# A recurrent scan with a top-1 mixture of experts on one core: second matrices kept on chip and addressed through a TensorE register

## The chip, the cores and the metric

The kernel runs on one core of one Trainium2 chip. The metric is the device time of one execution in microseconds (us). The times of the kernel before are the median, lowest and highest of three runs. The trace is of one more execution, taken by the hardware profiler.

## The reference, cut to what matters

```python
# part 1: x, r_gate, i_gate are 4 x 5056 x 256
a_t = exp(8 * sigmoid(r_gate) * log(sigmoid(a_param)))
x_gated = sqrt(max(1 - a_t*a_t, 1e-6)) * sigmoid(i_gate) * x
h[t] = a_t[t] * h[t-1] + x_gated[t]          # along the 5056 steps
# part 2: the 20224 rows of h (256 wide), 8 experts of 256 -> 1024 -> 256
e = argmax(h @ w_gate);  p = softmax(h @ w_gate)[e]
out = p * (relu(h @ w1[e]) @ w2[e])
```

## The kernel before, in words

The 20224 tokens are 158 blocks of 128, taken in 40 quads of up to four blocks. The program goes through these steps, with the names that its functions, and the lines below, have.

**Front of a quad.** ScalarE (ACT) computes tanh, exp and square root (L638 to L666), VectorE (DVE) multiplies and scans along time (L655, L671, L690). TensorE (PE) forms the gate logits (`lp`, L709), turns them (`lt`, L724) and transposes the scanned rows (`yt`, L747). ACT and DVE write each row as two fp16 parts, high and low (`hi` L774, `lw` L781), into `rows`.

**Routing.** Quads are taken in groups (`GROUPS`). For one group DVE finds each token's expert and gate weight (`r1` to `r6`, L796 to L857), PE counts places (`rk`, L815 and L816), and GpSimd (POOL) sends each block's rows with an indirect DMA to the region of their expert in `buf` in DRAM (`scat`, L870). A fence on SyncE (SP) tells that a group has landed.

**Slots.** The experts then work on slots of 256 or 128 rows of one expert. SP loads meta data and, by a DMA transpose, the rows (`xL`, L1061 and L1068). PE multiplies with the first matrix (`L1`, L1110), ACT applies relu (L1122), DVE makes the low part (L1130), PE multiplies with the second matrix (`L2`, L1149 to L1151), ACT scales (`ot`, L1160), and POOL stores the rows with an indirect DMA (`store`, L1171). In fp16 each product has three terms, high by high, high by low and low by high; this gives 48 matmuls for L1 and 48 for L2 in a slot of 256 rows (256 columns each), and 48 of 128 columns with 24 of 256 columns in a slot of 128 rows.

**The first eight slots, one for each expert,** are called raw: they use the fp32 matrices as they came, 32 and 32 matmuls in the trace (L1110, L1147) for 256 rows. The rows of the first two (`PICK = 2`) don't come by way of DRAM: DVE makes selection matrices for each block of the first four quads (`sel`, L892), PE multiplies them with `rows` (`pick`, L904), and ACT copies the product out of PSUM (`xs`, L910). The other six are read back from `buf`, and POOL joins their two parts (L1081). Meanwhile each of the 16 matrices is prepared for fp16: a sum of its magnitudes on ACT or DVE (`wm`, L956), the scale (`wt` on PE, L962, and `ws`), the high part on ACT (`wh`, L976), the low part on DVE (`wl`, L981), and a store into `wscr` in DRAM (`wr`).

**Later slots** are taken from tables that the device computes, so which expert a slot has is known only in a register. For each slot SP loads both prepared matrices (1 MB each) from `wscr` at an address of its registers (L1038), unless the buffer holds that expert already; POOL multiplies the gate weights with the scales of both matrices (`f`, L1093). There are `NB = 4` pairs of buffers.

The order of every engine's instructions is fixed when the program is built, by a planner (`Plan`): it runs its own model of the engines, takes the ready task with the best priority (`URGE`, `PREP`, `EARLY` and others), and counts the buffers in `BUFS`. On the chip the engines then wait for each other through semaphores, and each engine works its list in order.

## Time and profile before

| | |
|---|---|
| median of 3 runs | 1061.1 us (1059.38 to 1061.73) |
| the profiled execution | 1071.31 us, its span 1069.5 us, mean granted TensorE clock 0.988 |
| PE busy | 990.3 us (93% of the span), 8854 matmuls recorded |
| weight loads of PE, DVE, ACT, POOL busy | 860.6, 688.3, 616.8, 422.4 us |
| moved by DMA | 305.72 MB, mean 286 GB/s |

The span is read in four stretches. Up to the first L1 at 80.6 us ACT and DVE work on the first four quads and PE waits. From there to about 225 us the raw slots run while matrices are prepared. From there to 1032 us the slots from the tables run while the other quads are scanned and routed. The last 37 us are slots alone, and the stores of the last rows.

### The profile page before, as it was taken

The page shows a single profiled execution, that of the slowest core. Times are in us where ns is not written, and L with a number is a line of the kernel's source. Part 1 is how long each engine was busy: PE and PEld are TensorE (multiplying, and loading weights), DVE is VectorE, ACT ScalarE, POOL GpSimd, SP SyncE. Part 2 cuts the span into 40 slices and gives each one's busy share as a digit, 9 for nine tenths or more (in the row PEclk, how much of TensorE's full clock was granted, in tenths as well). Part 3 has the DMA queues.
Part 4 walks back from the last instruction along what each step waited for, and adds up shares of the span by engine and source line. Part 5 has one row for each costly group of instructions (what it writes and reads, how often), then busy time and mean ns, then how long its engine had stood idle before and what let it go on. Part 6 is the DMA issues. An engine that isn't in the chain of part 4 may idle for free. (4 is left out here: it accounts for less than half of the span.)

```text
span 1069.5 us, 23793 instructions
## 1 busy us (share of the span) xinstructions
PE 990.3 (93%) x8854; PEld 860.6 (80%) x8854; DVE 688.3 (64%) x1448; ACT 616.8 (58%) x815; POOL 422.4 (39%) x498
## 2 busy tenths in 40 slices
PE   1369898989899999999999999999999999999997
PEld 1138787878778888888888888888888888889987
DVE  4898898886676666758667585765858464422221
ACT  8988785664837466664755747466674632222222
POOL 0154454333446434353544525345253434222222
PEclk9979999999999999999999999999999999999999
DMA  9977998989998989799899989969899997878881
GB/s 366 380 241 213 324 336 282 299 281 327 331 332 245 316 275 356 208 343 308 263 323 309 345 267 316 295 199 350 303 348 297 279 316 195 238 241 267 224 245 54
DMA packets 167028, 305.72 MB, mean 286 GB/s; under 512 B 117621, under 2 KB 117754, under 8 KB 145659
## 3 DMA queue, kind: packets, MB, share of 16 engines
q1 hardware_dynamic: 151450, 262.56, 77.5%
q0 software_dynamic: 15456, 41.60, 12.2%
q8 instruction: 70, 1.15, 0.4%
q14 instruction: 52, 0.42, 0.1%
HBM read 251.48 MB, written 63.91 MB: 295 GB/s over the span
## 5 line engine op out<-in xcount | busy, mean ns | idle before, releaser
L1110 PE MATMUL p<-xT,wt 128*128 128x256 f16 (+1 forms) x3936 | 414.7, 263 | 8.3 <-DMA wt<-wscr 6.1
L1110 PEld LDWEIGHTS <-wt 128*128 128x128 f16 x3936 | 353.9, 98 | 48.1 <-DMA wt<-wscr 6.9
L1130 DVE SCALAR_TENSOR_TENSOR hb<-p,hb 128x1024 f16<-128x1024 f32 x148 | 180.7, 1221 | 238.7 <-ACT hb L1122 217.9
L1171 POOL DMA_INDIRECT out<-ot,meta x164 | 179.4, 1094 | 383.6 <-ACT ot L1160 340.8
L1149 PE MATMUL po<-wt,hb 128*128 128x256 f16 x1184 | 322.8, 273 | 7.9 <-ACT ot L1160 6.9
L1150 PE MATMUL po<-wt,hb 128*128 128x256 f16 x1184 | 322.8, 273 | 0.9 <-issue 0.9
L1151 PE MATMUL po<-wt,hb 128*128 128x256 f16 x1184 | 322.8, 273 | 0.1
L1122 ACT ACTIVATE hb<-p 128x1024 f16<-128x1024 f32 (+1 forms) x164 | 167.0, 1018 | 206.6 <-PE p L1110 170.0
L870 POOL DMA_INDIRECT buf<-rows,pi x158 | 169.7, 1074 | 49.3 <-issue 35.0
L1160 ACT ACTIVATE ot<-po,f 128x256 f32<-128x256 f32 x148 | 69.7, 471 | 170.5 <-PE po L1151 110.5
L1150 PEld LDWEIGHTS <-hb 128*128 128x128 f16 x1184 | 115.8, 98 | 22.9 <-issue 9.5
L1149 PEld LDWEIGHTS <-hb 128*128 128x128 f16 x1184 | 115.7, 98 | 15.5 <-issue 1.3
L1151 PEld LDWEIGHTS <-hb 128*128 128x128 f16 x1184 | 115.8, 98 | 14.5 <-issue 1.1
L690 DVE TENSOR_TENSOR_SCAN in_x<-in_r,in_x 128x512 f32<-128x512 f32 (+7 forms) x82 | 96.6, 1189 | 1.3
L1093 POOL TENSOR_SCALAR f<-meta,wt,wt 128x2 f32<-128x2 f32 (+1 forms) x82 | 38.3, 468 | 130.3 <-DMA wt<-wscr 93.8
L781 DVE SCALAR_TENSOR_TENSOR rows<-yt,sc,rows 128x256 f16<-128x256 f32 x154 | 65.3, 476 | 5.3 <-ACT rows L774 2.6
L655 DVE SCALAR_TENSOR_TENSOR in_x<-in_i,in_x 128x1024 f32<-128x1024 f32 (+1 forms) x38 | 46.0, 1214 | 34.8 <-ACT in_i L649 26.3
L774 ACT ACTIVATE rows<-yt,sc 128x256 f16<-128x256 f32 x154 | 61.9, 475 | 5.0 <-DVE sc L766 5.0
L1147 PE MATMUL po<-wt,hb 128*128 128x256 f32 x256 | 63.3, 398 | 0.9 <-ACT ot L1158 0.7
L671 DVE SCALAR_TENSOR_TENSOR in_x<-in_i,in_x 128x1024 f32<-128x1024 f32 (+1 forms) x38 | 45.6, 1200 | 24.9 <-ACT in_i L666 22.9
L1110 PE MATMUL p<-x,wt 128*128 128x256 f32 x256 | 58.3, 382 | 0.7 <-ACT x L910 0.7
L1147 PEld LDWEIGHTS po<-wt,hb 128*128 128x128 f32 x256 | 49.0, 198 | 8.7 <-ACT ot L1158 1.5
(126 smaller groups left out, 912.0 us busy)
## 6 DMA issues: line engine op xcount, KB each, us to landing
wt<-wscr SPq DMA_DIRECT2D x164, 1024.5 KB
in_x<-in_rix SPq DMA_DIRECT2D x39, 512.0 KB
in_r<-in_rix SPq DMA_DIRECT2D x37, 512.0 KB
in_i<-in_rix SPq DMA_DIRECT2D x37, 512.0 KB
wscr<-hl SPq DMA_DIRECT2D x16, 1024.5 KB
wt<-in_w SPq DMA_DIRECT2D x16, 1024.0 KB
out<-ot,meta POOLq DMA_INDIRECT x164
buf<-pad SPq DMA_DIRECT2D x10, 258.0 KB
```

Of the source, the lines that this page charges most:

```text
L690: V.tensor_tensor_scan(y[:, lo:hi], av[:, lo:hi], y[:, lo:hi], init, ALU.mult, ALU.add)
L781: V.scalar_tensor_tensor(r[:, 2 * p + j, D:2 * D], o["yt", p][:, j], o["sc"][:, 2 * p + j:2 * p + j + 1], r[:, 2 * p + j, 0:D], ALU.mult, ...
L870: i = G.indirect_dma_start(out=buf[:, :], out_offset=bass.IndirectOffsetOnAxis(ap=g["pi"][:, b0 + j:b0 + j + 1], axis=0), in_=rows[q]["row ...
L1110: T.matmul(pv[:, i], wv[:, wl, kk, fs], o["xT"][:, 2 * xl + kk, 0:U], start=(z == 0), stop=(z == len(seq) - 1))
L1122: A.activation(o["h"][:, gs, 0:U] if o["raw"] else o["h"][:, 0, gs, 0:U], o["p1", g], AF.Relu)
L1130: V.scalar_tensor_tensor(o["h"][:, 1, gs, 0:U], o["p1", g], 0.0, o["h"][:, 0, gs, 0:U], ALU.max, ALU.subtract)
L1147: T.matmul(dst, h[:, f, ts], wv[:, f, :], start=(f == 0), stop=(f == NF - 1))
L1149: T.matmul(dst, h[:, 0, f, ts], wv[:, 0, f, :], start=(f == 0), stop=False)
L1150: T.matmul(dst, h[:, 0, f, ts], wv[:, 1, f, :], start=False, stop=False)
L1151: T.matmul(dst, h[:, 1, f, ts], wv[:, 0, f, :], start=False, stop=(f == NF - 1))
L1160: A.activation(o["ot", j], o["po", j], AF.Copy, scale=o["f2"][:, j:j + 1])
L1171: i = G.indirect_dma_start(out=out[:, :], out_offset=bass.IndirectOffsetOnAxis(ap=o["id"][j], axis=0), in_=o["ot", j], in_offset=None, bou ...
```

## The change

**Second matrices.** All eight prepared second matrices lie side by side in one tile `w2all` on chip. For each slot PE itself loads the expert's number into one of its registers (`second`), and every matmul of L2 takes its moving operand at an address computed from that register (`times`). From `wscr` only the first matrix is loaded, 1 MB for a slot, into `NB = 5` single buffers; the scales of both matrices travel with it. A raw second matrix is loaded into the place of the next expert's prepared one.

**First slots.** The raw slots of experts 0 to 2 have 128 rows, picked from the first two quads alone (`NEAR = 3`, `PASSES`); experts 3 to 7 have 256 rows, read from `buf` after quads 2 and 3. The picking has 32 matmuls of 384 columns (before 64 of 512) and 24 selection matrices of 128 columns for a quad (before 16 of 256).

**Elsewhere.** `GROUPS` are all of two quads; the sums `wm` of nine matrices are on ACT (before six), each in two halves; fewer buffers for several tiles (`rows` 4 to 2, `xT` 4 to 2, `ot` 9 to 2, `hl` 2 to 1, `x32` 6 to 3); other priorities, hence another order on every engine.

```diff
-NB = 4
+NB = 5
-PASSES = ((1, 256, 8),)
+PASSES = ((0, 128), (1, 256), (2, 256))
-SUMS = (0, 6)
+SUMS = (0, 9)
-PICK = 2
+NEAR = 3
...
-BUFS = dict(r=3, i=4, x=6, rows=4, yt=2, lp=1, rank=1, tot=1, lg=4, hl=2, xT=4, hb=3, ot=9, po=1, p1=2, reg=3, x32=6)
+BUFS = dict(r=3, i=2, x=4, rows=2, yt=2, lp=1, rank=1, tot=2, lg=4, hl=1, xT=2, hb=3, ot=2, po=1, p1=2, reg=3, x32=3)
...
-            cond = None if was is None or was[1] else o["er"] != was[0]
-            nc.sync.dma_start(t, wscr[bass.ds(o["er"], 1), i].rearrange("a p c -> p (a c)"), cond=cond)
+        nc.sync.dma_start(t, wscr[bass.ds(o["er"], 1)].rearrange("a p c -> p (a c)"), cond=None if was is None else o["er"] != was)
+
+    def second(o):
+
+        z = st["tab", o["z"]]["ti"][:, 0, o["j"]:o["j"] + 1]
+        o["ep"] = nc.values_load(z, engines=[mybir.EngineType.PE], min_val=0, max_val=E - 1, skip_runtime_bounds_check_because="an expert")
+
+    def times(o, dst, h, l, f, **kw):
+        x = T.matmul(dst, h, w2all[:, bass.ds(o["ep"], 1), (l * NF + f) * D:(l * NF + f + 1) * D].rearrange("p a d -> p (a d)"), **kw)
...
-            T.matmul(dst, h[:, 0, f, ts], wv[:, 0, f, :], start=(f == 0), stop=False)
-            T.matmul(dst, h[:, 0, f, ts], wv[:, 1, f, :], start=False, stop=False)
-            T.matmul(dst, h[:, 1, f, ts], wv[:, 0, f, :], start=False, stop=(f == NF - 1))
+            times(o, dst, h[:, 0, f, ts], 0, f, start=(f == 0), stop=False)
+            times(o, dst, h[:, 0, f, ts], 1, f, start=False, stop=False)
+            times(o, dst, h[:, 1, f, ts], 0, f, start=False, stop=(f == NF - 1))
...
-    wts = [[wpool.tile([P, 4 * F + 2], F16, name=f"wt{i}{z}") for z in range(NB - 1)] for i in range(2)]
+    wts = [wpool.tile([P, 4 * F + 4], F16, name=f"wt{z}") for z in range(NB - 1)]
+    w2all = wpool.tile([P, E, 4 * F], F16, name="w2all")
```

The order changes on every engine; three places follow. The first is PE, before, at the beginning of the second product of a slot from the tables: `hb` is the relu's output (the stationary operand), `wt` a buffer of matrices, `po` the sum in PSUM.

```order
L1149 LDWEIGHTS hb
L1149 MATMUL po<-wt_141,hb 128x256
L1150 LDWEIGHTS hb
L1150 MATMUL po<-wt_141,hb 128x256
L1151 LDWEIGHTS hb
L1151 MATMUL po<-wt_141,hb 128x256
```

The same place after the change, where `ti` is the table in SBUF, and ISA is the register instruction that works out the address:

```order
L1120 MATMUL p_8660<-xT,wt_133 128x256
L1046 LDWEIGHTS hb
L1043 TENSOR_LOAD ti
L1046 ISA
L1046 MATMUL po<-w2all,hb 128x256
L1046 LDWEIGHTS hb
L1046 ISA
L1046 MATMUL po<-w2all,hb 128x256
```

One register load comes into each slot, and one register instruction between every weight load and its matmul of L2: 48 in a slot of 256 rows and 24 in one of 128, 3624 in the slots that are executed.

The second place is ACT ahead of the copies of the picked rows. Before (L956 and L976 are `wm` and `wh`, L910 the copies):

```order
L956 ACTIVATE hl,wm<-wt_137 128x2048
L660 ACTIVATE in_i<-in_r 128x1024
L666 ACT_TABLE_LOAD
L666 ACTIVATE in_i<-in_i,quarter 128x1024
L976 ACTIVATE hl<-wt_140,wsc 128x2048
L666 ACTIVATE in_i<-in_i,quarter 128x1024
L649 ACT_TABLE_LOAD
L649 ACTIVATE in_i<-in_i 128x1024
L910 COPY x_659<-p_375 128x512
L910 COPY x_661<-p_375 128x512
```

After (L660 is the square root of quad 3; L948 is `wm`, L980 `wh`, L906 the copies):

```order
L660 ACTIVATE hb<-hb,quarter 128x1024
L948 ACTIVATE junk,wm_358<-wt_132 128x1024 x2
L948 ACTIVATE junk,wm_382<-w2all 128x1024 x2
L948 ACTIVATE junk,wm_397<-wt_133 128x1024 x2
L948 ACTIVATE junk,wm_418<-w2all 128x1024 x2
L948 ACTIVATE junk,wm_439<-w2all 128x1024 x2
L980 ACTIVATE hl<-wt_131,wsc 128x2048
L710 COPY ls<-misc 128x128
L980 ACTIVATE w2all<-w2all,wsc 128x2048
L906 COPY x_494<-p_400 128x2x128
L906 COPY x_497<-p_400 128x2x128
L906 COPY x_525<-p_400 128x2x128
```

The copies now follow the square root of quad 3 with five sums and two conversions between, and the fronts of quads 4 and 5, which stood ahead of them, come behind.

The third place is POOL after the scatters of quad 3. Before (L870 scatter, L1081 join, L1166 and L1171 the scaling and store of a picked slot's rows):

```order
L870 DMA buf<-rows,pi 166400x258 x4
L1081 ISA
L1081 TENSOR_TENSOR x_780<-xT 128x512
L1081 TENSOR_TENSOR x_802<-xT 128x512
L1081 TENSOR_TENSOR x_832<-xT 128x512
L1166 TENSOR_SCALAR ot<-ot,meta 128x256
```

After (L864 scatter, L1091 join, L1179 and L1184 scaling and store):

```order
L864 DMA buf<-rows,pi 166400x258 x4
L1184 DMA out<-ot,meta 20224x256
L1179 TENSOR_SCALAR ot<-ot,meta 128x256
L1184 DMA out<-ot,meta 20224x256
L1179 TENSOR_SCALAR ot<-ot,meta 128x256
L1184 DMA out<-ot,meta 20224x256
L1091 TENSOR_TENSOR x_866<-xT 128x512
L1091 TENSOR_TENSOR x_899<-xT 128x512
```

The first join, for the first slot whose rows come by way of DRAM, now stands behind the stores of all three picked slots.

## Rows read from the trace of the kernel before

**Rows 1.** Busy time by stretch: from and to, length, then busy us (and instructions) of PE, its weight loads, DVE, ACT and POOL, the granted clock as a share of full speed, the busy share of the DMA engines and GB/s.
```profile
0.00:80.60 80.60, 31.65 (x176) 16.27 (x176) 62.07 (x157) 72.11 (x85) 19.89 (x26) 0.92 0.89 330
80.60:110.00 29.40, 29.11 (x153) 24.64 (x154) 24.93 (x37) 25.89 (x29) 13.46 (x11) 1.00 0.82 209
110.00:300.00 190.00, 176.44 (x1200) 151.19 (x1200) 156.09 (x295) 124.53 (x156) 86.27 (x93) 0.97 0.96 314
300.00:1032.00 732.00, 723.35 (x6968) 641.55 (x6966) 439.11 (x957) 385.90 (x536) 293.18 (x357) 1.00 0.92 285
1032.00:1055.50 23.50, 21.62 (x291) 20.25 (x291) 4.90 (x4) 5.93 (x10) 4.36 (x7) 1.00 0.51 162
1055.50:1069.50 14.00, 8.10 (x72) 6.70 (x69) 1.22 (x1) 2.39 (x4) 5.27 (x7) 0.96 0.10 36
```

**Rows 2.** The waits of PE from 104 to 1032 us: who waited for whom, us in total, times, longest.
```profile
PE po L1149 <- ACT ot L1160: 5.1, 9, 1.3
PE p L1110 <- DMA wt<-wscr: 4.3, 2, 3.1
PE yt L747 <- DVE rows L781: 3.8, 2, 2.2
PE misc L709 <- DVE hl L969: 3.0, 1, 3.0
```

**Rows 3.** The timeline of PE around the first slots: start, us, engine, line, operation, names, shapes, count, and in brackets the idle time before it.
```profile
80.62 3.72 PE L1110 MATMUL p<-x,wt 128*128 128x256 f32 x16 [0.68 <-ACT x L910]
...
93.52 3.70 PE L1147 MATMUL po<-wt,hb 128*128 128x256 f32 x16
...
104.54 3.62 PE L1110 MATMUL p<-x,wt 128*128 128x256 f32 x16
```

**Rows 4.** The timeline of ACT from 46 to 76 us, same columns.
```profile
46.78 1.28 ACT L644 ACT_TABLE_LOAD   x1
...
51.29 1.15 ACT L666 ACTIVATE hb<-hb,quarter 128x1024 f32<-128x1024 f32 x1
...
65.31 1.93 ACT L956 ACTIVATE hl<-wt 128x2048 bf16<-128x2048 f32 x1
67.11 0.22 ACT L956 ACTIVATION_READ_ACCUMULATOR hl<-wt 128x1 f32 x1
...
73.80 1.99 ACT L976 ACTIVATE hl<-wt,wsc 128x2048 f16<-128x2048 f32 x1
```

**Rows 5.** The timeline of POOL from 70 to 97 us, same columns.
```profile
70.02 0.19 POOL L864 COPY rows<-fa 128x4 f32<-128x4 f32 x1 [9.29 <-DVE fa L857]
70.85 0.98 POOL L870 DMA_INDIRECT buf<-rows,pi  x1 [0.64 <-ACT hl L956]
72.14 1.03 POOL L870 DMA_INDIRECT buf<-rows,pi  x1 [0.30 <-issue]
...
83.58 1.01 POOL L870 DMA_INDIRECT buf<-rows,pi  x1 [0.30 <-ACT in_r L644]
96.05 1.15 POOL L1081 TENSOR_TENSOR x<-xT 128x512 f32<-128x512 f16 x1 [11.47 <-DMA xT<-buf]
```

**Rows 6.** The preparation of the matrices and the end of the raw slots, by line: instructions, shortest, median and longest in ns, start of the first and of the last.
```profile
L981 DVE SCALAR_TENSOR_TENSOR hl<-wt,wsc,hl x16: 2323/2340/3135, 32.8 to 225.6; 128x2048 f16<-128x2048 f32 x16
L1160 ACT ACTIVATE ot<-po,meta x12: 457/473/474, 129.7 to 221.9; 128x256 f32<-128x256 f32 x12
```

**Rows 7.** The timeline of PE in two later stretches: two successive L1 halves of 24 matmuls in slots of 256 rows, with 24 of L2 between, and two successive L1 of slots of 128 rows.
```profile
412.06 2.79 PE L1110 MATMUL p<-xT,wt 128*128 128x256 f16 x24
417.30 2.78 PE L1110 MATMUL p<-xT,wt 128*128 128x256 f16 x24
...
996.45 2.84 PE L1110 MATMUL p<-xT,wt 128*128 128x128 f16 x48
1001.75 2.84 PE L1110 MATMUL p<-xT,wt 128*128 128x128 f16 x48
```

**Rows 8.** Transfers issued by SP: the loads of prepared matrices, count and KB of each.
```profile
wt<-wscr SPq DMA_DIRECT2D x164, 1024.5 KB
```

**Rows 9.** Register instructions ahead of one load on SP, piece by piece in the chain that ended last: start, us, what.
```profile
1032.18 0.04 issue
1032.22 0.06 SPq L1038
1032.28 0.05 issue
```

**Rows 10.** The same line over the whole run: its instructions that reckon in registers, shortest, median and longest in ns.
```profile
L1038 SPq FUSED_REGOPS  x242: 2/56/688, 192.9 to 1043.1; - x121
```

**Rows 11.** The one place before where PE's sequencer loads a register from SBUF, by line; it is followed by a branch.
```profile
L1292 PEldq TENSOR_LOAD <-used x1: 483/483/483, 1026.3 to 1026.3; - x1
```

**Rows 12.** The timeline of PE behind that load.
```profile
1028.14 0.27 PE L1151 MATMUL po<-wt,hb 128*128 128x256 f16 x1
...
1028.72 1.00 PE L1110 MATMUL p<-xT,wt 128*128 128x128 f16 x15 [0.30 <-PEq L1293]
```

**Rows 13.** Who waited for the stores (us, times), from the view of that line.
```profile
  ACT ot L1160: 14.0, 8
```

**Rows 14.** The chain that ended last, at the last store: start, us, what.
```profile
1063.23 2.19 issue
```

## The prediction

> **What bounds the kernel now.** I read the stretches first [rows 1]. Up to the first slot at 80.6 us PE is busy 31.65 us, so it waits 49 us: this stretch belongs to ACT (72.1 us busy) and DVE (62.1). From 110 to 300 us PE misses 13.6 us of 190, from 300 to 1032 us 8.6 of 732, from 1032 to 1055.5 us 1.9 of 23.5. Behind 80 us PE is thus the bound, and a transfer, load or register step counts only where PE waits for it. The waits come next [rows 2]: from 104 to 1032 us PE waits 5.1 us for the scaling of outputs, 4.3 for loads of matrices, 3.8 for DVE's low parts and 3.0 for DVE's scale factors. That is all a cheaper load could give back on PE, although the DMA engines are busy 0.92 to 0.96 of the time. The last view is the rate [rows 7]: 24 matmuls of L1 and 24 of L2 take 417.30 − 412.06 = 5.24 us, 0.109 each; a slot of 256 rows takes 96 × 0.109 = 10.48 us. A slot of 128 rows takes 1001.75 − 996.45 = 5.30 us, of which 24 × 0.109 = 2.62 are L2, and 2.68 are 48 matmuls at 55.8 ns.

> The profiled execution took 1071.3 us, 10.2 more than the median of 1061.1. I sum against 1071.3 and take 10.2 off.

> **PE's own work: −6.0 us.** In rows handled nothing changes: 8 × 256 raw, 66 × 256 and 16 × 128 prepared are 20992, and 3 × 128 + 5 × 256 raw, 68 × 256 and 15 × 128 prepared, counted in the new order, are 20992 too. A raw slot is four pieces of 16 matmuls of about 3.62 us [rows 3], 14.5 us, half that for 128 rows. Raw work falls from 116.0 to 21.75 + 72.5 = 94.25 us, −21.7; prepared work gains 2 × 10.48 − 5.30 = 15.7.

> **The start: 0 us, −6 to +8.** ACT ends the square root of quad 3 at 51.29 + 1.15 = 52.4 us [rows 4]. In the new order two conversions (1.99 each) and two table loads (1.28) that stood ahead of it are gone: about 45.9. Behind it stand five sums at 1.93 + 0.2 and two conversions, about 14.7 us, then the copies. The first L1 can begin at about 61.5 instead of 80.62, 19 us earlier. That isn't 19 us gained. Three slots of 7.25 us last until about 83; the fourth needs rows by way of DRAM. The gate values of quads 2 and 3, ready at 70.0 [rows 5], now come behind two conversions of 2.34 us on DVE [rows 6], two sums there, and the first relus on ACT: 75 to 79. Two quads of scatters at 1.29 us a block take 10.3 us or a little more, so they end at 86 to 90. From the last scatter's end to the end of the first join was 83.58 + 1.01 = 84.6 to 96.05 + 1.15 = 97.2, 12.6 us. The fourth slot starts at 99 to 103, 105 if PE's list holds it behind quads 4 and 5. Before, six raw pieces, the same 21.7 us, were done at 104.54 [rows 3]. So PE is where it was, with an idle gap of some 15 to 20 us in the first 105, and I take 0. What does come earlier is preparation: five sums and two conversions are done by 61.

> **Waits between 105 and 1032 us: −9.8 us.** With one load of 1 MB for a slot in place of up to two (164 loads were issued [rows 8]), PE's 4.3 us for loads go, since five single buffers hold more than a slot's lead. The 3.0 us for DVE's scale factors go with the earlier sums. Of the 5.1 us for the scaled output I take half: it waits for the gate weights times the scales, and these for loads. The 3.8 us for low parts stay, since `rows` has two buffers in place of four. −4.3 − 3.0 − 2.5 = −9.8; the bounds are 0 and all of PE's idle time there, 13.6 + 8.6 = 22.2 us.

> **Fewer buffers: +2 us, 0 to 15.** ACT waited 14.0 us for stores with nine output buffers [rows 13]. A store takes about 1 us and then 2.19 until it has landed [rows 14], with the scaling (0.47 [rows 6]) 3.7 us; two buffers are taken once in 10.48 us. That is enough while POOL is free, but a quad's scatters hold it 4 × 1.29 = 5.2 us. I take 2; were all of ACT's 14 us passed on to PE it would be 14.

> **Register instructions on PE: +4 us, 0 to 41.** No row shows a matmul with a register address. 48 pairs of L1 pass at 55.8 ns [rows 7], so a pair needs at most that of the sequencer; call it 30 to 55.8. A register step on SP took 56 ns [rows 10], with 0.04 to 0.05 us of issue around it [rows 9]. A triple of weight load, register step and matmul then takes between 55.8 (the step lies beside the rest) and 55.8 + 56 + 45 = 157 ns; if the matmul has to be handled as slowly as the step, some 200. Its time on the array is 109, so L2 alone falls behind, and L1 gives the lead back. The load of the register took 483 ns [rows 11], once a slot, while queued matmuls went on: after it at 1026.3 they ran at their rate to 1028.14, so some 17 pairs were queued [rows 12]. In a slot of 256 rows the sequencer needs 0.5 + 48 × 0.045 + 48 t, and 10.48 hides it up to t = 163 ns (152 with pairs at 55.8). In a slot of 128 rows it is 0.5 + 48 × 0.045 + 24 t against 5.30: hidden up to 110 ns. I take t = 120, nearer to the sum of step and pair, 112, than to the end with gaps: 0.24 us × 15 = 4 us; at 157 it is 17 us, and with pairs at 55.8 as well 25 + 16 = 41 us, the upper bound.

> [...]

> **The tail: 0.** The last chain is stores on POOL with their landing; they stay.

> **Sum.** −6.0 + 0 − 9.8 + 2 + 4 = −9.8: 1061.5 for a profiled run, 1051 for the median.

> **Rivals.** *The sequencer becomes the bound (slower).* Place: L2 of every prepared slot, between weight load and matmul. Above 163 ns each ns costs 48 × 68 slots = 3.3 us, and 15 × 24 = 0.4 more in the small slots. Slower begins where it costs 15 us or more, about 155 ns. At 165 ns it is 7 + 20 = 27 us, 1061.1 − 13.8 + 27 = 1074; at 180, 81 us and 1128. For it: step and gaps as SP has them give 157. Against it: a queue of 17 pairs or more, and L1's share of each slot. *Larger gain.* The fourth slot starts at 95, since scatters before took only 1.29 us a block, and earlier preparation removes another 6 of the 13.6 us that PE misses from 110 to 300: −9.5 − 6, 1036. For it: DMA is freed of up to half the loads and landing gets shorter. Against: the fourth slot's chain through fence, transposes and join has no DMA load of matrices in it to remove. *A wash.* Two `ot`, `rows` and `xT` buffers pass their waits to PE: 12 us rather than 2, 1061. For it: the 14.0 us even with nine buffers; against: ACT's wait was rarely PE's. *The change does not do what it says*: fewer loads bring nothing because PE's waits for them had another cause; then 4.3 + 2.5 stay and the time is 1058, inside the forecast's range.

> **How the numbers follow.** Forecast 0.48, own range 1041 to 1059; larger gain 0.18; wash 0.12; sequencer 0.22, half of it under 1085. The range from 1034 to 1082 leaves out some 0.1 above and 0.05 below. A difference under 0.2% (2.1 us) can't be told from none by a measurement of this kernel. Faster: 0.46 + 0.18 + 0.03 = 0.67; same: 0.07, nearly all from the wash; slower: 0.26, with 0.22 from the sequencer and the rest from the wash.

> **What would show it.** Right: the first L1 near 61 us, a gap of PE ahead of the fourth slot which starts near 103; L2 of prepared slots at 109 ns a matmul with no idle; loads of 1 MB about half as many; no wait of PE for them. If L2's matmuls stand further apart than 109 ns, or PE idles for its own sequencer at the turn to L2, the register term is wrong. If PE waits longest for outputs or low parts, the buffers are. If the fourth slot starts under 97 or over 110, the start is. The forecast falls if the slots of 256 rows take over 10.7 us.

## The result and the profile after

The kernel after took a median of 1068.4 us (five runs, 1067.5 to 1069.9), the kernel before 1061.1 beside it (1058.0 to 1064.4): a ratio of 1.0073, 95% interval 1.0047 to 1.0098. The forecast was 1051 and faster; the kernel became slower, by more than the 0.2% that a measurement can tell. The profiled execution took 1069.1 us, its span 1067.3, against 1071.3 and 1069.5 before: by the two profiles alone it is 2.2 us shorter. The ratios here and below leave out executions in a slower state of the chip, so they need not be the quotients of the medians given.

Four rows of the page after: busy time, two DMA queues (packets, MB, share), and, of the costliest groups, L2.

```profile
PE 987.5 (93%) x8910; PEld 863.6 (81%) x8910; DVE 674.5 (63%) x1405; ACT 621.8 (58%) x837; POOL 432.3 (41%) x497
q1 hardware_dynamic: 143480, 192.44, 61.3%
q8 instruction: 86, 1.41, 0.5%
L1046 PE MATMUL po<-w2all,hb 128*128 x3624 | 428.8, 272 | 3.8 <-ACT ot L1173 3.8
```

The loads of matrices, which answer to [rows 8], and the register steps of L2:

```profile
wt<-wscr SPq DMA_DIRECT2D x83, 1025.0 KB
```

```profile
L1046 PEldq FUSED_REGOPS  x3624: 51/55/60, 204.9 to 1062.2; - x191
```

Half of the loads are gone (83 for 164), and 3624 steps of 55 ns have come. By stretch, with the columns of [rows 1]:

```profile
85.00:110.00 25.00, 8.91 (x49) 6.35 (x49) 18.99 (x23) 18.56 (x19) 14.30 (x12) 0.61 0.77 221
...
300.00:400.00 100.00, 100.00 (x927) 88.10 (x926) 69.64 (x148) 61.02 (x83) 47.49 (x59) 1.00 0.80 234
400.00:600.00 200.00, 200.00 (x1865) 176.62 (x1863) 138.99 (x299) 118.92 (x165) 85.33 (x101) 1.00 0.80 236
...
1000.00:1067.30 67.30, 54.41 (x633) 46.99 (x630) 10.38 (x9) 13.39 (x19) 13.50 (x18) 0.94 0.23 62
```

The middle is what was hoped for: from 300 to 600 us PE misses nothing. The last stretch isn't: 12.9 us of 67.3 are lost. The waits of PE from 105 to 1032 us, against [rows 2], have a new piece:

```profile
PE misc L809 <- DVE oh L801: 7.2, 1, 7.2
PE p L1120 <- PEq L1310: 6.7, 1, 6.7
PE yt L741 <- DVE rows L775: 3.0, 2, 2.7
PE po L1046 <- ACT ot L1173: 2.4, 1, 2.4
PE p L1120 <- DMA wt<-wscr: 2.2, 1, 2.2
```

The first row is PE's gap ahead of the fourth slot, to which the part on the start comes back. The second row is new: 6.7 us, once, for PE's own sequencer at L1310. That is the jump over the guarded remainder, the code for slots of the last table beyond the sure ones, which isn't executed with these data. Before it stood at L1293. The same view of that line, before and after:

```profile
L1293 PEldq COMPARE_BRANCH  x1: 418/418/418, 1026.9 to 1026.9; - x1
L1310 PEldq COMPARE_BRANCH  x1: 6262/6262/6262, 1017.8 to 1017.8; - x1
```

PE's timeline around it, with the columns of [rows 3]:

```profile
1012.03 2.84 PE L1120 MATMUL p<-xT,wt 128*128 128x128 f16 x48
1014.71 2.98 PE L1046 MATMUL po<-w2all,hb 128*128 x24
1024.41 4.99 PE L1120 MATMUL p<-xT,wt 128*128 128x128 f16 x48 [6.72 <-PEq L1310]
1029.24 2.78 PE L1046 MATMUL po<-w2all,hb 128*128 x24
1031.86 2.84 PE L1120 MATMUL p<-xT,wt 128*128 128x128 f16 x48
```

A slot of 128 rows takes about 5.55 us here; the one with the jump takes 12.38 from L1 to L1, and the next 7.45, since its L1 lasts 4.99 us instead of 2.84. The stretches from 1017.70 us on show PE's standstill and then the granted clock (the third number from the end) in that L1, 0.52:

```profile
1017.70:1024.40 6.70, 0.00 (x0) 0.02 (x1) 0.00 (x0) 0.47 (x1) 1.36 (x2) 0.83 0.56 178
1024.40:1029.20 4.80, 4.79 (x48) 4.80 (x49) 0.00 (x0) 0.00 (x0) 0.00 (x0) 0.52 0.03 4
```

So the jump costs 6.8 + 1.9 = 8.7 us here.

The table shows where the time went between the two profiles, with the slots' own time (14.5, 10.48 and 5.30 us, as in the prediction) taken out of each stage. In both kernels two L1 halves of prepared slots (2 × 2.62 us) run before the last product of the raw slots, and they count with the second stage:

| stage | before | after | difference | forecast |
|---|---|---|---|---|
| to the end of the raw slots | 100.5 | 104.1 | +3.6 | 0 |
| PE's own work in slots, by those durations | | | −6.1 | −6.0 |
| slots of 256 rows, the rest (66, then 68 slots) | 61.8 | 51.3 | −10.5 | −9.8 + 2 = −7.8 |
| slots of 128 rows to the last matmul, the rest (16, then 15) | 9.8 | 20.5 | +10.7 | +4, tail 0 |

Of the last row, the jump's two slots hold 7.08 + 2.15 us above 5.30, against 3.1 for the three slots from the jump on before: +6.1. Those 3.1 are not the jump alone: PE stood 0.30 us for it, then 0.50 for an output and 1.82 for a load, and whether these two hung on the jump isn't shown.

```profile
1032.06 0.27 PE L1149 MATMUL po<-wt,hb 128*128 128x256 f16 x1 [0.50 <-ACT ot L1160]
...
1041.96 2.85 PE L1110 MATMUL p<-xT,wt 128*128 128x128 f16 x48 [1.82 <-DMA wt<-wscr]
```

The other +4.6 is 0.2 to 0.3 us on most of the remaining slots and 1.8 on the last products.

### The profile page after: what moved, and what is told of

Read it like the earlier page. It is cut to its first block, busy times and chain, and to the rows that moved or that the text cites. A ratio compares the mean times of both kernels' runs of the same rounds, so it can differ in the third digit from the quotient of the medians.

```text
span 1067.3 us, 27279 instructions
## 1 busy us (share of the span) xinstructions
PE 987.5 (93%) x8910; PEld 863.6 (81%) x8910; DVE 674.5 (63%) x1405; ACT 621.8 (58%) x837; POOL 432.3 (41%) x497
## 4 chain that ended last, share of the span: by engine, by line
PE 75%; DMA 10%; issue 8%; ACT 2%; DVE 2%; POOL 2%; SPq 0%; POOLq 0%; DVEq 0%; ACTq 0%
PE p L1120 36%; PE po L1046 32%; PE yt L741 3%; PE po L1160 3%; DMA out<-ot,meta 2%; DMA w2all<-in_w 2%; DMA xT<-buf 2%; PE misc L703 2%; DMA wscr<-hl 1%; POOL out L1184 1%; DMA buf<-rows,pi 1%; DMA hb<-in_rix 1%; DVE hl L985 1%; ACT junk L948 1%; DMA cst<-in_c 1%
## 5 line engine op out<-in xcount | busy, mean ns | idle before, releaser
L1046 PE MATMUL po<-w2all,hb 128*128 x3624 | 428.8, 272 | 3.8 <-ACT ot L1173 3.8
L1184 POOL DMA_INDIRECT out<-ot,meta x164 | 177.9, 1085 | 462.6 <-ACT ot L1173 443.5
L864 POOL DMA_INDIRECT buf<-rows,pi x158 | 180.3, 1141 | 53.9 <-issue 32.2
L748 DVE TENSOR_REDUCE m<-yt 128x2 f32<-128x512 f32 x79 | 51.6, 682 | 18.4 <-PE yt L741 18.4
L741 PE MATMUL yt<-cst,in_x 128*128 128x128 f32 x316 | 48.0, 293 | 13.9 <-DVE in_x L684 5.5
L1120 PE MATMUL p<-x,wt 128*128 128x256 f32 (+1 forms) x256 | 52.3, 366 | 1.8 <-ACT x L906 1.8
L741 PEld LDWEIGHTS yt<-cst,in_x 128*128 128x128 f32 x316 | 38.1, 150 | 19.4 <-issue 11.7
L703 PE MATMUL misc<-in_x,wg 128*32 128x256 f32 (+1 forms) x360 | 24.7, 389 | 29.0 <-DVE in_x L684 27.5
L1120 PEld LDWEIGHTS p<-x,wt 128*128 128x128 f32 x256 | 45.2, 212 | 6.5 <-ACT x L906 2.0
L1103 POOL TENSOR_SCALAR f<-meta,wt 128x2 f32<-128x2 f32 (+1 forms) x83 | 35.4, 427 | 31.9 <-DMA meta<-buf 16.9
L638 ACT ACTIVATE in_r<-in_r,k 128x1024 f32<-128x1024 f32 (+2 forms) x42 | 48.0, 1146 | 0.4
```

The costliest lines, as they stand in the source:

```text
L741: T.transpose(t[:, j, h * P:(h + 1) * P], part(q, h, "x")[:, (2 * p + j) * P:(2 * p + j + 1) * P], ident)
L748: V.tensor_reduce(o["m"][:, 2 * p:2 * p + 2], o["yt", p], AX.X, ALU.max, apply_absolute_value=True)
L864: i = G.indirect_dma_start(out=buf[:, :], out_offset=bass.IndirectOffsetOnAxis(ap=g["pi"][:, b0 + j:b0 + j + 1], axis=0), in_=rows[q]["row ...
L1046: x = T.matmul(dst, h, w2all[:, bass.ds(o["ep"], 1), (l * NF + f) * D:(l * NF + f + 1) * D].rearrange("p a d -> p (a d)"), **kw)
L1120: T.matmul(pv[:, i], wv[:, wl, kk, fs], o["xT"][:, 2 * xl + kk, 0:U], start=(z == 0), stop=(z == len(seq) - 1))
L1184: i = G.indirect_dma_start(out=out[:, :], out_offset=bass.IndirectOffsetOnAxis(ap=o["id"][j], axis=0), in_=o["ot", j], in_offset=None, bou ...
```

## The experiments

The theories: the jump over the remainder, not the register steps, costs the tail (R); the place of the jump in PE's code decides its price (P); the register steps cost more than 4 us (the first rival of the prediction); the late fourth slot costs PE time (the start). The runs are from four chips; the kernel before took 1084.2 us on that of e1 to e4, 1068.6 on that of e5 to e8, 1086.9 on e9 to e12's and 1088.6 on e13 to e15's. Each ratio is against the kernel before on the same chip.

**The kernel before, again.** No edit.

> The kernel before, unchanged, as a control for the 10.2 us that lay between its profiled execution (1071.3 us) and its timed median (1061.1). If the profiler as such costs this kernel 10 us, its profiled execution is again some 10 us above its timed runs. If that one execution was merely a long one, the new profiled execution lies within 4 us of the timed runs, and the waits of PE from 110 to 1032 us are then fewer than 22 us, about 12 to 16.

1082.6 us, ratio 1.0002 (0.9967 to 1.0038). Its profiled execution took 1074.4, which is 8.2 *below* its median; in the prediction's profile it was 10.2 above. The offset is not a property of being profiled. Nor was the first profile one with more waits: from 110 to 1032 us PE is idle 22.2 us in it and 24.1 in e1, though on another chip.

**Without the remainder, and without register steps.**

```diff
-            tc.mark_branch_hint_location("few", engines=[mybir.EngineType.PE])
-            rest()
+            pass
```

and in e3 besides

```diff
-        x = T.matmul(dst, h, w2all[:, bass.ds(o["ep"], 1), ...
+        x = T.matmul(dst, h, w2all[:, 0:1, ...
-                second(o)
+                o["ep"] = 0
```

> The changed kernel without the guarded remainder (44 less 15 slots that these data don't use) and without the prefetch hint for its branch; the output stays whole for these data. Theory R: PE lost 6.7 us of idle time and some 2 us at a low clock because its jump over that remainder had to wait for code. Then the time falls by 7 to 9 us, to about 1060, and the slots of 128 rows follow each other without a gap. Rival: PE would have waited there anyway for SP, whose own jump took 5.8 us, or for loads behind it; then the time falls by 0 to 3 us.

> As e2, and L2 reads the second matrix of expert 0 at a fixed address: no register load, no register instruction (this leaves out the choice of the expert's second matrix). Register theory: each slot of 128 rows goes from 5.58 back to 5.30 us, 15 times 0.28, 4.2 us in all, and slots of 256 rows stay at 10.48, so 4 us below e2. Rival: register instructions also cost in slots of 256 rows, which the trace after shows at 200.00 of 200 us busy; then it falls by more than 8 us.

e2 took 1101.2 us, ratio 1.0125 (1.0063 to 1.0186): the changed kernel itself wasn't run on this chip, so what e2 gained on it isn't known. e3 took 1073.3, 0.9889 (0.9844 to 0.9934). From the first slot of 128 rows to the last matmul e2 needed 90.7 us, e3 86.7: the register steps cost 4.0 there, as forecast. But the whole difference is 27.9 us, and by the profiles 21.3 of it lie in the slots of 256 rows and 2.7 ahead of them. The waits of PE in e2 from 300 to 960 us:

```profile
PE po L1046 <- ACT ot L1173: 6.1, 6, 1.4
PE p L1120 <- issue: 5.8, 15, 0.9
PE po L1046 <- issue: 4.1, 10, 0.9
```

In 25 places PE stops for nothing that the profile shows; in the profile after, on the first chip, no such row stands in this stretch. Behind a stop successive matmuls of L2 mostly start 132 to 134 ns apart, not 109; that a stop leaves no queued matmuls, and that L1 gives the lead back, is the author's reading. e2 has 333 pairs of starts 115 to 150 ns apart in the 256-row stage, the first chip's profile 51. An estimate for the whole stage: stops take 11.1 us in e2 and 5.3 in e3, and 333 × 24 ns are 8.0, together 13.8 of the 21.3; the rest isn't assigned.

**Loads issued twice.** Each load of a first matrix has a second copy of itself behind it.

> The changed kernel with every load of a first matrix from DRAM issued twice into the same buffer, so the bytes of the kernel before are moved again (about 2 MB a slot). If the waits of PE between 117 and 960 us went because of the halved loads, 6 to 15 us come back, to 1075 to 1083. Rival: they went because of the new order and the earlier preparation; then it stays within 3 us of 1068.4.

1338.1 us, ratio 1.233 (1.226 to 1.24). PE waits 33.7 us for rows (`xT`) and 155.4 for outputs; that SP's queue stands behind the second copy, which waits for the first, is the author's reading and not shown. The run says nothing of bytes alone: a failed experiment, and so no run shows that the halved loads are what took PE's waits away.

**The remainder on a chip like the first.** The changed kernel, and e2's edit.

> The changed kernel, unchanged, as a control on the chip of this call. In e1 to e3 the chip gave 1084 us for the kernel before, not 1061, and PE idled there in bursts of some 0.5 to 1 us (50 of them, 26.6 us, in e2) for which the profile shows no releaser. If the change costs the same everywhere, the ratio is 1.007 again. If what it costs hangs on how fast a chip brings instructions, it is 1.00 to 1.03, and the larger the more such bursts the profile shows.

> As e2, now beside the changed kernel on one chip. Theory R (PE's jump over the guarded remainder waits for code): 7 to 9 us below e5, with PE's idle 6.7 us at the jump gone. Rival (SP's own jump would hold the slots anyway): within 3 us of e5.

e5: 1075.5 us, 1.005 (1.0029 to 1.0072); e6: 1065.2, 0.9961 (0.9934 to 0.9988). e6 is 10.3 us below e5 and faster than the kernel before. The tail took 100.5 and 90.5 us; the jump in e5 6.38. R holds: on such a chip the remainder and its jump cost the changed kernel more than it loses to the kernel before. But the kernel before keeps its own remainder in this comparison, whose three slots from the jump on cost it 3.1 us, so which kernel would be faster without either remainder isn't shown.

**Another place for the jump.** 64 matmuls of 16 columns at the start of PE's program, 95 in e10 and e14; their result isn't used.

```diff
+            for _ in range(64):
+                T.matmul(po[:, 0:16], umat, umat[:, 0:16], start=True, stop=True)
```

> The changed kernel with 64 more matmuls of 16 columns (128 PE instructions) at its very beginning, where PE idles; their result is overwritten. If the place of the jump in the code decides whether its target is there in time, the jump takes under 1 us on PE, as in the kernel before, and the time falls by 6 to 9 us. If the length of the remainder decides, the jump takes 6 us as in e5 and the time stays within 2 us.

1073.4 us, 1.0013 (0.9989 to 1.0037), 2.1 below e5. The branch itself took 0.42 us, but PE stopped a little behind its target:

```profile
1027.31 1.78 PE L1120 MATMUL p<-xT,wt 128*128 128x128 f16 x29 [0.88 <-PEq L1310]
1032.48 2.21 PE L1120 MATMUL p<-xT,wt 128*128 128x128 f16 x19 [3.39 <-issue]
```

A code packet of 16,384 bytes starts on q8 3.6 us behind the branch, takes 1.06, and the stop ends 1.2 us later. In the author's reading the packet fits a target that was there and a continuation that wasn't, and a further shift should put both in reach:

> As e7 with 95 added matmuls in place of 64. In e7 the jump took 0.42 us instead of 6.4, but 29 pairs behind its target PE stood still for 3.4 us more. If code comes in pieces of 256 instructions and e7's target lay some 60 instructions before the end of its piece, 62 more instructions put the target just behind a border: the jump stays under 1 us, the stop of 3.4 us goes, and the time is 4 to 6 us below the changed kernel (ratio 0.999 to 1.001). If the stop was SP's jump and not PE's code, it stays, and the ratio is e7's 1.001 to 1.004.

1113.4 us, 1.0233 (1.0183 to 1.0284), on a chip of the other sort, where the ratio can't be held against either forecast; the tail took 92.2 us, the jump 0.42. The next three stand side by side on one chip: the changed kernel, the shifted one, and the changed kernel without the marker that announces the jump.

> The changed kernel as it is, beside the next two on the same chip. Both theories: the jump over the guarded remainder takes 6.2 to 6.4 us on PE, 100 us from the first slot of 128 rows to the last matmul. Its ratio to the kernel before is 1.005 to 1.008 on a chip like the first one, 1.01 to 1.03 on the other sort.

> The changed kernel with 95 small matmuls at the start of PE's program (their result is not used), which only shifts the place of the jump in PE's code. Theory P (the place of the jump and of its target in PE's code decides): the jump takes about 0.42 us, the tail 92 us instead of 100, and the run is 7 to 9 us shorter than the one before it here, about 0.993 of it. Rival (the gain of the tail is an accident of that one chip, or comes back elsewhere): within 3 us of the run before it.

```diff
-        if t is soon:
-            tc.mark_branch_hint_location("few", engines=[mybir.EngineType.PE])
```

> The changed kernel without the marker that announces the jump to PE ahead of time; the jump and the guarded remainder stay. Removing it takes an instruction or two out of PE's code as well, so the place hardly moves. Theory P: the marker brings nothing where the jump stands badly; 6 to 7 us at the jump as before, within 2 us of the first run here. Rival H (the marker itself fetches the wrong piece, or throws out one that PE needs): the jump falls under 4 us and the run is 3 to 6 us shorter. Rival N (the marker saves something even there): 8 us or more at the jump, 2 us or more longer.

e13: 1114.5 us, 1.0249 (1.0204 to 1.0293). e14: 1107.8, 1.0182 (1.0126 to 1.0239). e15: 1115.7, 1.0245 (1.0191 to 1.03). The branch row of e13, then of e14, and e14's timeline at the jump:

```profile
L1310 PEldq COMPARE_BRANCH  x1: 6267/6267/6267, 1059.9 to 1059.9; - x1
```

```profile
L1310 PEldq COMPARE_BRANCH  x1: 422/422/422, 1063.0 to 1063.0; - x1
```

```profile
1063.76 2.84 PE L1120 MATMUL p<-xT,wt 128*128 128x128 f16 x48 [0.94 <-PEq L1310]
```

The tails are 99.8, 92.3 and 100.2 us, so the shift gives back 7.5 us where it was looked for; of the whole time e14 is 6.8 us below e13 by the means of six runs each, with a standard error of 2.7. P holds. At this place the marker makes no difference that shows (6.30 us without it). No run has a cheap place without the marker, so whether the cheap price needs it stays open. PE executes the marker's instruction at its very beginning:

```profile
L1406 PEldq BRANCH_PREFETCH_HINT  x1: 50/50/50, 0.8 to 0.8; - x1
```

The trace also has a sign of what PE waits for. In the profile after, q8, taken here for the queue of PE's code, moves nothing from 1009.5 to 1017.8 us; from 1017.8 to 1024.1, the jump's stretch, it has one packet:

```profile
q8 instruction: 1, 0.02, 1.0%
```

It starts 3.8 us into the jump and takes 1.05, and the jump ends 1.4 us later. In all six runs with a dear jump the packet starts 3.7 to 3.9 us into it; what fills those us isn't shown. In e14 the last packet ahead of the jump came 4.6 us before it, but in e4, where the jump is as cheap, 9.5 us, the same as in the profile after. The recorded instructions of PE ahead of the jump, counted modulo 256, are 193 to 195 in all six runs with a jump of 6.1 to 6.4 us, and 66, 118, 127, 128 and 192 in those with 0.4 to 0.5. The last of these is e4: one recorded instruction less than e9, and the jump is cheap. The two differ in their loads and their order too, so this pair suggests a border between 192 and 193 and doesn't prove it. The 256 is read from the trace: q8's packets are all of 16,384 bytes, and ahead of the jump they start 256.0 recorded instructions of PE apart in the mean of 79 intervals in the profile after, 257.1 in the mean of 65 in the one before. The author's estimate, from that and from the packet inside each of the six dear jumps, is that PE waits there for a piece of its code. This doesn't explain the cheap ones: by the kernel's text the remainder has 29 slots (44 less 15) of some 170 PE instructions, about 4900 or 19 such packets, and if they lie between jump and target, the target is as far off where the jump is cheap.

**The start.** e8 and e9 move 17 and 20 tasks of the order, so that the fourth slot's rows are written and read earlier; e11 is e9 with the 95 matmuls. The core of the edit:

```diff
     plan = Plan(batch, seq)
+    for what, side, target in [(('yt', (3, 1)), 1, ('yt', (3, 0))), ...]:
+        x = plan.ops.pop(...);  plan.ops.insert(... + side, x)
```

> The changed kernel with 17 tasks moved in its list, nothing added: on PE the second transpose of quad 3 ahead of slot 2, and slot 3's first L1 ahead of the logits of quads 4 and 5; on DVE and ACT quad 3's rows and the gate values ahead of the fronts of quads 4 and 5; a low part (expert 1, second matrix) behind the scatters; on ACT slot 2's output copy ahead of the conversions that wait for a store; on POOL the first join ahead of slot 2's store. Start theory: slot 3 began at 116.6 because of that order; now it begins at 100 to 106 and 9 to 14 us stay gained at the end. Rival 1: the landing of the scatters among other transfers holds it, and it begins at 110 or later, gain under 5. Rival 2: it begins early, but later slots then wait for prepared matrices, and less than half of it is left at the end.

> e8 mended in the place where it failed: there ACT stood still from 88.8 to 105.2 us, because with two output buffers slot 2's copy waits until slot 0's store has landed, and that store came behind the scatters. Now that store comes right behind its scaling, before the scatters, and the fence stands in SP's list ahead of a load for quad 6. Start theory: slot 3 begins at 100 to 108 instead of 116.6, and 7 to 14 us stay gained at the end against the changed kernel (ratio 0.992 to 0.998 to the kernel before). Rival: the scatters land 8 to 10 us after their issue as in e5, slot 3 begins at 110 or later and the ratio stays at 1.003 or more.

> e9 and e10 together, the version that is to beat both kernels. If the two are independent their gains add: 11 to 20 us below the changed kernel, ratio 0.986 to 0.996. If start gains are given back later, it is e10 within 3 us.

e8: 1095.7 us, 1.0236 (1.0204 to 1.0267). The store of a picked slot had moved behind the scatters, both `ot` buffers were taken, and ACT stood:

```profile
105.23 0.37 ACT L1171 COPY ot<-po 128x256 f32<-128x256 f32 x1 [16.39 <-DMA out<-ot,meta]
```

e9: 1127.7 us, 1.0358 (1.031 to 1.0405). The fourth slot did start earlier, at 109.5 instead of 116.6 us, but the fifth later:

```profile
109.50 9.19 PE L1120 MATMUL p<-x,wt 128*128 128x256 f32 x32 [5.75 <-POOL x L1091]
...
136.30 1.44 PE L959 MATMUL misc<-wm,ones 128*128 128x1 f32 x6 [3.41 <-DVE inv L967]
137.60 2.91 PE L1120 MATMUL p<-x,wt 128*128 128x256 f32 x6
```

In e10, the changed kernel with its jump shifted on the same chip, the fourth began at 116.8 and the fifth at 125.8. The first slot from the tables began at 211.7 us in e9, against 200.3 in e10. e11: 1115.1 us, 1.0248 (1.0199 to 1.0296), no better than e10 beside it. What the fourth slot gains is taken from the fronts: PE forms the logits of quads 4 and 5 behind its L1 now, and DVE stands waiting for PE:

```profile
119.76 0.16 DVE L967 SCALAR_TENSOR_TENSOR inv<-misc,wtop 128x2 bf16<-128x2 f32 x1 [14.87 <-PE misc L703]
```

So these runs reject this order, not every earlier fourth slot.

**Register steps, again.** e3's edit, beside e10.

> As e3 (no remainder, L2 at a fixed address, which leaves out the choice of the expert's second matrix), on the chip of this call. On the chip of e5 to e8 the kernel without the remainder had the ratio 0.9961; its profile shows 66 matmul gaps of 0.115 to 0.15 us (1.4 us), 15 slots of 128 rows 0.28 us late (4.2 us) and 2.6 us of longer gaps. Register theory: the ratio is 0.4 to 0.7% lower, 0.989 to 0.992. If register instructions cost some 25 us on every chip, as between e2 and e3, it is 0.975 or lower.

1079.9 us, 0.9936 (0.9909 to 0.9963), 33.5 below e10; the stage of 256-row slots took 782.9 us against 811.5. The ratio lies just above the first forecast, but the distance to e10 has the size of the second: the first took its base, 0.9961, from a chip of the other sort than this one. The 33.5 include e10's remainder and its cheap jump.

## Why the prediction was wrong

*"The tail: 0"* is the step that failed. It looked at the last stores and left out the jump, although a line of [rows 12], read there for another figure, has the 0.30 us that PE waited at L1293. The change adds 3624 register steps to PE's code and removes or moves matmuls, so the same jump falls on another place in that code (194 recorded instructions ahead of it, modulo 256, where it was 118). It cost 8.7 us with the clock that it took along (9.2 above 5.30 a slot), against 3.1 for the three slots from the jump on before, of which PE's wait at the jump is 0.30. e6 and the pair e13 and e14 show it: without the remainder the changed kernel takes 10.3 us less, and with the jump shifted 6.8 less.

*"I sum against 1071.3 and take 10.2 off"* is the second, and by its size the larger. The forecast for a profiled run was 1061.5, and it came to 1069.1: 7.6 us, of which the tail is 6.7, the start 3.6 and waits and buffers −2.7. Nearly all the rest of the 17.4 between 1051 and 1068.4 is the offset, 9.5 us: it was 10.2 before and is 0.7 after. One execution of a kernel whose runs scatter was taken for a constant; e1 had it at −8.2. The step assumed that the profiled waits of before were also those of its median run. Where the timed runs before spent 10 us less isn't shown, since none of them has a trace.

*PE's own work* (−6.0): 68 and 15 slots ran as counted, and the table takes the durations over without testing them. *The waits and buffers* gave more than forecast (−10.5 for −7.8): loads halved, PE's wait for them is 2.2 us for 4.3, the wait for outputs 2.4 for 5.1, the wait for scale factors 0.3 for 3.0.

*The start* stayed within its range (+3.6) and was wrong in its steps. The first L1 began at 60.7 (61.5 forecast), but the fourth slot at 116.6, not 99 to 103. The scatters of quads 2 and 3 ended at 98.0, not 86 to 90: the gate values came at 80.8 us, not 75 to 79, POOL's small copies ahead of the scatters, 0.19 us in [rows 5], took 2.3 each, two of the scatters 1.7 and 2.0, and the join 2.40 where it took 1.15:

```profile
80.82 2.26 POOL L858 COPY rows<-fa 128x4 f32<-128x4 f32 x1 [1.58 <-DVE fa L851]
...
88.87 2.31 POOL L858 COPY rows<-fa 128x4 f32<-128x4 f32 x1
...
113.43 2.40 POOL L1091 TENSOR_TENSOR x<-xT 128x512 f32<-128x512 f16 x1
```

In DVE's timeline two of the low parts stand beside the two copies:

```profile
80.68 2.35 DVE L985 SCALAR_TENSOR_TENSOR w2all<-w2all,wsc 128x2048 f16<-128x2048 f32 x1
...
88.81 2.34 DVE L985 SCALAR_TENSOR_TENSOR hl<-wt,wsc,hl 128x2048 f16<-128x2048 f32 x1
```

Then 17.8 us, not 12.6, passed from the last scatter to the end of the first join. Up to the fence it is 9.3 us (to 107.29), where it was 6.5 before (to 91.07):

```profile
91.07 0.25 SPq L915 DMA_DIRECT2D fence<-buf  x1
...
107.29 0.25 SPq L911 DMA_DIRECT2D fence<-buf  x1
```

The clock, too, was left out: after PE's gap the first 16 matmuls of the fourth slot took 5.79 us instead of 3.62, at a granted clock of 0.62, and the first 64 of the raw slots some 10 instead of 7 at the rate of the third slot, at 0.72:

```profile
60.71 10.12 PE L1120 MATMUL p<-x,wt 128*128 128x128 f32 x64 [1.83 <-ACT x L906]
...
116.62 5.79 PE L1120 MATMUL p<-x,wt 128*128 128x256 f32 x16
```

*The register steps* were sized well for the chip that was measured: t was taken as 120 ns, and where L2's matmuls start more than the array's 109 ns apart it is 133 (in the slots of 128 rows of the profile after 124 gaps are 130 to 136 ns, of 134 from 115 to 150); 0.24 us a small slot were forecast, and 0.2 to 0.3 came, with 1.8 on the last products. That is luck in part: the longer t is set off by the load of the register, which took 0.30 us where 0.48 was taken. The 256-row slots hid them, as 100.00 us busy of 100 shows. The 133 ns lie above the 55.8 at which the step would have lain beside the pair and below the plain sum, 157. For a pair of L1 itself, taken there as 30 to 55.8 ns and then as 45, the trace shows the 55.8 alone. On two of the three chips of the other sort (the third has no such pair) the rival's bounds were the better guide: 27.9 us (e2 less e3) and 33.5 (e10 less e12, remainder included), inside the 41. It isn't a sequencer slower than the array everywhere, though: the matmuls are spread behind stops, which account for part of it.

*What stays open.* Why the jump takes only 0.4 to 0.5 us at other places. What the stops are. They stand in the "issue" rows, come in bursts, and more of them in kernels with register steps (28 of PE in e2 from 215 to 1005 us, 12 in e3 from 215 to 980). In one burst of e2, from 405 to 413 us, no packet came on q8, and ACT and DVE were busy for only 3.7 and 1.9 us, so late code is not shown to be the cause. Why chips differ in it isn't shown either.

## What to carry to other kernels

When a change alters the number of an engine's instructions, price every jump on that engine anew, also one that the change doesn't touch (here PE's went from 0.42 to 6.26 us): look for its row in the trace, and if the engine stands there, shift the code and measure again. Forecast a difference between two executions of one kind, and give the offset between a profile and a median a range of its own. An address from a register cost PE nothing in the slots of 256 rows that ran without a stop (100.00 us busy of 100 in the profile after), and 24 ns a matmul behind a stop (133 for 109 in e2), so price it at the stops too.
